# A third row buffer in the raw slots of the last expert's weights, used from the fifth unit on

## The chip, the core and the metric

The kernel runs on one core of one Trainium2 chip. Its five engines (TensorE for matmuls, VectorE and ScalarE for element-wise work, GpSimd, which here issues indirect DMAs, and SyncE, which here issues plain DMAs and transposing loads) each take their instructions in a fixed order and wait for each other through semaphores. In the rows below they are PE (PEld: its weight loads), DVE, ACT, POOL and SP. The metric is the device time of one execution in microseconds (us); lower is better.

## What is computed

A causal convolution over 7 steps with softmax weights per head, and behind it a mixture of experts: each of 28672 tokens of width 192 goes to its two best of eight experts, with hidden width 1024.

```
w = softmax(weight)                                   # 8 heads, 7 taps
x = sum over k of w[h, k] * x_pad[:, s + k, h, :]     # 8 x 3584 tokens of 192
logits = x @ w_gate
noisy_logits = logits + log1p(exp(x @ w_noise)) * noise
top2, top2_w = two largest, softmax of the two
for e in range(8):
    h = maximum(x[mask] @ w1[e], 0.0)                 # 192 -> 1024
    out[mask] += top2_w[mask] * (h @ w2[e])           # 1024 -> 192
```

## The kernel before

**Units.** The tokens are cut into 28 units of 1024 (128 partitions by 8 tokens). A unit's way has four steps. Its x is loaded (`load_x`, two buffers) and convolved by the thread `conv`: 56 VectorE operations into `xc` (L574, L576; TensorE does it for the first units, L528). Then `xc` is scaled and written as two f16 parts, high and low, into a **row buffer** `rb`: ScalarE writes the high part (L599 and L601), VectorE the low part (L603 and L605). The thread `gating` transposes the rows (eight transposing DMAs on SP, L636, from unit 5 on), computes the logits (L651), picks the two experts, and writes weights and token number into the last columns of the same rows. Last, `scatters` sends every row to its place in two experts' lists in DRAM (`xs`): 16 indirect DMAs on GpSimd (L783). When the sixteenth has landed, the row buffer is free.

**Row buffers.** There are two (`NRB`), so unit u writes where unit u - 2 was. L595 and L596 tell the planner so (`mark("scattered", u - NRB)`), and on the chip L599 waits on the semaphores of those scatters. Each buffer has a pad that is set to zero once (L433).

**Blocks.** The other half of the work is 232 blocks: 29 rounds of eight experts. A block of 256 rows (128 in the first round) is loaded transposed from `xs` (`bT`, three buffers, L938 and L941 on SP), multiplied by w1 (L858, into `ph`), passed through relu into `h` (high part on ScalarE, L881; low part on VectorE, L885), multiplied by w2 (L895, 24 matmuls for 128 rows, into the one `py`), scaled by ScalarE into `y` (L902, six buffers) and added to the output by an indirect DMA on GpSimd (L907). One 128-row half is one y and one add. The adds of a block wait until those of the block before have landed. A round needs the scattered rows of certain units, and a small load of their numbers (L803) ahead of its first block.

**Order.** No engine's order comes from the code as it stands. A planner (`Plan`) runs all these parts as threads against estimated durations, and records an instruction on its engine when its thread is the next to go. `conv` and `gating` have an urgency that grows as the unit's round comes near (`due`); the scatters are spread out over time on purpose (at most 2.6 us plus 1.4 us each). A thread that meets a mark not yet set stands still in the plan.

**Weights.** Each expert's weights are loaded raw in four parts and split into an f16 high and low part (`split_weights`, L424 on ScalarE and L426 on VectorE). The slots form two chains: the split of one part is written into the slot in front of its raw one (`parts`). `slots1` and `slots2` have 17 slots each, of 1024 and 768 f32 per partition, and the two in the last places hold raw weights of the last expert only. Behind its split they are not used again.

Of the kernel before, what the change touches and what calls it, by code (L numbers as in the profile page):

```python
# [8 lines left out]
F32 = mybir.dt.float32  # L9
F16 = mybir.dt.float16  # L10
# [8 lines left out]
P = 128  # L19
TU = 8  # L20
ROW = 400
ROWF = ROW // 2
# [110 lines left out]
def kernel(  # L133
# [12 lines left out]
    B, S, D = x.shape  # L146
    H, K = weight.shape
    G = D // H
    E, _, F = w1.shape
# [26 lines left out]
    const = ctx.enter_context(tc.tile_pool(name="const", bufs=1))  # L176
# [19 lines left out]
    V = nc.vector  # L196
# [41 lines left out]
    def pow2(mx, n, t, name):  # L238

        f = small.tile([P, n], I32, name=name + "f")  # L240
        s = small.tile([P, n], I32, name=name + "s")
        i = small.tile([P, n], I32, name=name + "i")
        V.tensor_scalar(f, mx.bitcast(I32), 23, None, op0=OP.logical_shift_right)
        V.tensor_scalar(f, f, -1, t + 254, op0=OP.mult, op1=OP.add)
        V.tensor_scalar(f, f, 1, 253, op0=OP.max, op1=OP.min)
        V.tensor_scalar(s, f, 23, None, op0=OP.logical_shift_left)
        V.tensor_scalar(f, f, -1, 254, op0=OP.mult, op1=OP.add)
        V.tensor_scalar(i, f, 23, None, op0=OP.logical_shift_left)
        return s.bitcast(F32), i.bitcast(F32)
# [13 lines left out]
    PE, DVE, ACT, SP, POOL = "PE", "DVE", "ACT", "SP", "POOL"  # L263
# [4 lines left out]
    def mark(*key):  # L268
        return marks.setdefault(key, Mark())

    def done(*key, after=0.0):
        plan.mark(mark(*key), after)
# [23 lines left out]

    HC = FC // 2
    winv = const.tile([P, E], F32, name="winv")
    slots1 = [const.tile([P, F], F32, name=f"w1s{n}") for n in range(2 * E + 1)]
    slots2 = [const.tile([P, HC * D], F32, name=f"w2s{n}") for n in range(2 * E + 1)]  # L300

    def parts(e, c):
        slots, n = ((slots1, 2 * e + c), (slots2, 2 * e + c - 2))[c // 2]
# [122 lines left out]
                V.scalar_tensor_tensor(lo, st, wscale[e][:, m:m + 1], hi, op0=OP.mult, op1=OP.subtract)  # L426
            done("split", e, m)

    NRB, NPE, NTR = 2, 3, 5
    rbs = []  # L430
    for i in range(NRB):
        rb = rpool.tile([P, TU, ROW], F16, name=f"rb{i}")
        V.memset(rb[:, :, 384:ROW], 0.0)  # L433
        rbs.append(rb)
    NPART = U // 2 if U % 2 == 0 else U
    nzt, cps, xcs, inv = {}, {}, {}, {}
    scat, zeroed = {}, []
# [121 lines left out]
    def conv():  # L559
        for u in range(U):  # L560
            turn["conv"], xc = u, None
            yield mark("x", u)
            if u:
                yield mark("halo", u)
            hs = range(H) if u >= NPE else range(HH, H) if u == 0 else range(0)
            for k in reversed(range(K)):
                for h in hs:
                    yield DVE, 0.25 if k == K - 1 else 0.33
                    if xc is None:
                        xc = xcs[u] = cpool.tile([P, TU, D], F32, name="xc")  # L570
                    src = xts[u][:, k:k + TU, h * G:(h + 1) * G]
                    dst = xc[:, :, h * G:(h + 1) * G]
                    if k == K - 1:
                        V.tensor_scalar(dst, src, wt[:, h, k:k + 1], None, op0=OP.mult)  # L574
                    else:
                        V.scalar_tensor_tensor(dst, src, wt[:, h, k:k + 1], dst, op0=OP.mult, op1=OP.add)  # L576
            for h0 in range(0, H if u < NPE else 0, HH):
                if (u, h0) != (0, HH):
                    yield mark("cps", u, h0)
                    yield ACT, 0.95  # L580
                    if xc is None:
                        xc = xcs[u] = cpool.tile([P, TU, D], F32, name="xc")
                    nc.scalar.activation(xc.rearrange("p t (h g) -> p h t g", g=G)[:, h0:h0 + HH],  # L583
                                         cps[u, h0][:, :, :TU * G].rearrange("p h (t g) -> p h t g", g=G), AF.Copy)
                    plan.freed(ph_ring)
            done("conv", u)
            yield DVE, 1.7
            am = small.tile([P, TU], F32, name="am")
            V.tensor_reduce(am, xc, axis=AX.X, op=OP.max, apply_absolute_value=True)  # L589
            yield DVE, 1.3  # L590
            xsc, xinv = pow2(am, TU, TX, "x")
            yield DVE, 1.7
            V.tensor_tensor(xc, xc, xsc[:, :, None].to_broadcast([P, TU, D]), op=OP.mult)  # L593
            inv[u] = xinv
            if u >= NRB:  # L595
                yield mark("scattered", u - NRB)  # L596
            rb = rbs[u % NRB]
            yield ACT, 1.1
            nc.scalar.activation(rb[:, :, 0:128], xc[:, :, 0:128], AF.Copy)  # L599
            yield ACT, 0.6  # L600
            nc.scalar.activation(rb[:, :, 256:320], xc[:, :, 128:192], AF.Copy)  # L601
            yield DVE, 1.2
            V.tensor_tensor(rb[:, :, 128:256], xc[:, :, 0:128], rb[:, :, 0:128], op=OP.subtract)  # L603
            yield DVE, 0.65
            V.tensor_tensor(rb[:, :, 320:384], xc[:, :, 128:192], rb[:, :, 256:320], op=OP.subtract)  # L605
            done("rows", u)

    def gating():
        for u in range(U):
            turn["gating"] = u  # L610
            yield mark("rows", u)
            xinv, rb = inv.pop(u), rbs[u % NRB]
            rbf = rb.bitcast(F32)
            xT = None
            if u:
                yield from zeros_and_noise(u)
# [78 lines left out]
            for k in range(2):  # L695
                m = small.tile([P, TU], F32, name=f"m{k}")
# [395 lines left out]
    plan.spawn(halos(), 0.3)  # L1092
    plan.spawn(conv_pe(), 0.2)
    plan.spawn(conv(), wanted("conv", 70.0))
    plan.spawn(prepare_gates(), 0.3)
    plan.spawn(scale_weights(), wanted_weights("scale", 12.0))
    for m in range(2):
        plan.spawn(split_weights(m), wanted_weights(m, 6.0))
    plan.spawn(gating(), wanted("gating", 45.0))
    plan.spawn(block_loads(), 1.5)  # L1100
    plan.spawn(run_blocks())
# [60 lines left out]
```

## Time and profile before

| | us |
|---|---|
| three timed runs | 2024.60, 2022.66, 2016.06 |
| median | 2022.66 |
| the profiled execution's own time | 2030.29 |
| its span in the trace | 2028.3 |
| TensorE busy | 1946.0 (96%) |
| VectorE busy | 1557.7 (77%) |
| GpSimd busy | 1263.0 (62%) |
| ScalarE busy | 804.2 (40%) |

The page gives for each engine the time in which at least one of its instructions ran. TensorE's matmuls overlap, so a group's length in the timeline is read from the start of one group to the start of the next. "Idle before" in the timelines is the time for which an engine stood still ahead of an instruction, with what ended it; a wait for several semaphores is put down to the one that came last by the profile, and where the engine named had long been done it was another, often a DMA. Mean granted clock of TensorE over the span: 0.986 of full speed.

### The profile page before, as it was taken

To read this page: it belongs to the slowest core of one execution; us is meant where nothing else is said; L and a number is where in the kernel's file an instruction comes from. 1 tells how busy PE (TensorE), PEld (TensorE's weight loads), DVE (VectorE), ACT (ScalarE), POOL (GpSimd) and SP (SyncE) were. 2 spreads that over 40 slices of the span, in tenths; PEclk is the share of its full clock that TensorE was granted. 3 is DMA by queue.
4 is the path that set the end of the run, shared out by engine and by line. 5 is a ranking of instruction groups with operands and counts; after the bars stand their busy time and mean duration, and the time that the engine had idled before them with its cause. 6 is when DMAs were issued, how large, how long until landed. Compare 5 with 4: busy or idle time off the path is not lost. (4 is left out here: it accounts for less than half of the span.)

```text
span 2028.3 us, 52446 instructions
## 1 busy us (share of the span) xinstructions
PE 1946.0 (96%) x21703; PEld 1785.3 (88%) x21703; DVE 1557.7 (77%) x4042; ACT 804.2 (40%) x1173; POOL 1263.0 (62%) x915
## 2 busy tenths in 40 slices
PE   7779999999999999999999999999989999999997
PEld 7668899898999999989989888899989999999996
DVE  7799899898998989989888887788778865333332
ACT  4464444333444444334433333334333333333332
POOL 0566776577666767676666667666666666633333
PEclk9889999999999999999999999999999999999999
DMA  8845566877787767677766676667766765444442
GB/s 242 220 101 102 111 130 116 151 134 117 130 138 133 121 116 140 117 134 127 133 122 111 113 131 124 115 112 125 115 115 96 115 113 91 85 59 64 58 58 37
DMA packets 521882, 236.99 MB, mean 117 GB/s; under 512 B 401304, under 2 KB 508824, under 8 KB 521505
## 3 DMA queue, kind: packets, MB, share of 16 engines
q1 hardware_dynamic: 433824, 142.72, 34.2%
q0 software_dynamic: 87200, 90.80, 30.0%
q8 instruction: 171, 2.80, 0.6%
q14 instruction: 79, 0.65, 0.1%
q10 hardware_dynamic: 608, 0.02, 0.0%
HBM read 40.12 MB, written 115.38 MB: 77 GB/s over the span
## 5 line engine op out<-in xcount | busy, mean ns | idle before, releaser
L907 POOL DMA_INDIRECT out_dram<-y,ids x456 | 762.8, 1673 | 534.5 <-ACT y L902 160.7
L858 PE MATMUL ph<-bT,w1s 128*128 128x256 f16 (+2 forms) x9280 | 994.3, 271 | 15.9 <-DMA bT<-xs 7.7
L895 PE MATMUL py<-w2s,h 128*128 128x192 f16 x10944 | 986.2, 247 | 22.4 <-ACT y L902 22.3
L895 PEld LDWEIGHTS <-h 128*128 128x128 f16 x10944 | 910.3, 98 | 61.1 <-issue 53.5
L858 PEld LDWEIGHTS <-w1s 128*128 128x128 f16 (+1 forms) x9280 | 786.5, 97 | 131.5 <-issue 40.3
L885 DVE SCALAR_TENSOR_TENSOR h<-ph,h 128x1024 f16<-128x1024 f32 (+1 forms) x464 | 557.8, 1202 | 340.1 <-ACT h L881 336.7
L881 ACT ACTIVATE h<-ph 128x1024 f16<-128x1024 f32 (+1 forms) x464 | 468.2, 1009 | 593.9 <-PE ph L858 577.5
L783 POOL DMA_INDIRECT xs<-rb,idx x448 | 498.5, 1113 | 212.3 <-issue 133.0
L576 DVE SCALAR_TENSOR_TENSOR xc<-xt,wt,xc 128x192 f32<-128x192 f32 x1224 | 420.3, 409 | 2.1 <-DMA xt<-zero 2.1
L902 ACT ACTIVATE y<-py,ga 128x192 f32<-128x192 f32 x456 | 191.8, 421 | 487.7 <-PE py L895 483.1
L528 PE MATMUL ph<-xt,dg 128*128 128x192 f32 x280 | 50.4, 339 | 13.9 <-DMA xt<-in_x_dram 11.7
L603 DVE TENSOR_TENSOR rb<-xc,rb 128x1024 f16<-128x1024 f32 x28 | 34.2, 1220 | 37.8 <-ACT rb L599 34.9
L528 PEld LDWEIGHTS ph<-xt,dg 128*128 128x128 f32 x280 | 47.4, 198 | 14.3 <-DVE dg L508 11.7
L599 ACT ACTIVATE rb<-xc 128x1024 f16<-128x1024 f32 x28 | 29.5, 1055 | 65.2 <-DMA xs<-rb,idx 35.2
L574 DVE TENSOR_SCALAR xc<-xt,wt 128x192 f32<-128x192 f32 x204 | 53.9, 328 | 1.3 <-DMA xt<-in_x_dram 0.7
L589 DVE TENSOR_REDUCE am<-xc 128x8 f32<-128x1536 f32 x28 | 48.9, 1748 | 4.2 <-ACT xc L583 3.7
L593 DVE TENSOR_TENSOR xc<-xc,xs 128x1536 f32<-128x1536 f32 x28 | 49.0, 1751 | 0.0
L687 DVE SCALAR_TENSOR_TENSOR t<-t,t 128x64 f32<-128x64 f32 x168 | 37.8, 225 | 5.3
L497 ACT ACTIVATE xt<-xt 128x1152 f32<-128x1152 f32 x27 | 31.2, 1154 | 0.0
L733 DVE TENSOR_REDUCE sums<-M 128x72 f16<-128x576 f16 x23 | 26.7, 1160 | 0.0
L651 PE MATMUL misc<-gparts,xT 128*128 128x32 f16 (+1 forms) x752 | 23.3, 174 | 1.4 <-DMA xT<-rb 1.4
L651 PEld LDWEIGHTS <-xT 128*128 128x128 f16 x752 | 22.7, 96 | 1.9 <-DMA xT<-rb 1.5
(142 smaller groups left out, 613.9 us busy)
## 6 DMA issues: line engine op xcount, KB each, us to landing
out_dram<-zero SPq DMA_DIRECT2D x28, 768.0 KB
xt<-in_x_dram SPq DMA_DIRECT2D x27, 768.0 KB
bT<-xs SPq DMA_TRANSPOSE x464
out_dram<-y,ids POOLq DMA_INDIRECT x456
xs<-rb,idx POOLq DMA_INDIRECT x448
w2s<-in_moe_w_dram SPq DMA_DIRECT2D x16, 384.0 KB
w1s<-in_moe_w_dram SPq DMA_DIRECT2D x8, 512.0 KB
w1s<-in_moe_w_dram SPq DMA_DIRECT2D x16, 256.0 KB
```

The source lines that it names most:

```text
L528: nc.tensor.matmul(c[:, h - h0, :TU * G].rearrange("p (t g) -> p t g", g=G), diag[h, k], xts[u][:, k:k + TU, h * G:(h + 1) * G], start=(k ...
L574: V.tensor_scalar(dst, src, wt[:, h, k:k + 1], None, op0=OP.mult)
L576: V.scalar_tensor_tensor(dst, src, wt[:, h, k:k + 1], dst, op0=OP.mult, op1=OP.add)
L589: V.tensor_reduce(am, xc, axis=AX.X, op=OP.max, apply_absolute_value=True)
L593: V.tensor_tensor(xc, xc, xsc[:, :, None].to_broadcast([P, TU, D]), op=OP.mult)
L783: s = nc.gpsimd.indirect_dma_start(out=xsf, out_offset=bass.IndirectOffsetOnAxis(ap=idx[:, k, t:t + 1], axis=0), in_=rbf[:, t, :], in_offs ...
L858: nc.tensor.matmul(ph[:, f, :T], w, x, start=opens and f // 2 not in banks[:i], stop=closes and f // 2 not in banks[i + 1:], skip_group_ch ...
L881: nc.scalar.activation(h[:, 0, half * nf:(half + 1) * nf, :T], ph[:, :, :T], AF.Relu)
L885: V.scalar_tensor_tensor(h[:, 1, hs, :T], ph[:, :, :T], 0.0, h[:, 0, hs, :T], op0=OP.max, op1=OP.subtract)
L895: nc.tensor.matmul(py[:, half, :D], h[:, a, f, ts], w2_part(e, lo, f), start=(n == 0), stop=(n == 3 * FC - 1), skip_group_check=True)
L902: nc.scalar.activation(y, py, AF.Copy, scale=gate)
L907: a = nc.gpsimd.indirect_dma_start(out=out, out_offset=bass.IndirectOffsetOnAxis(ap=ids, axis=0), in_=y, in_offset=None, compute_op=OP.add)
```

## The change

The two slots in the last places of `slots1` and `slots2` become two views of one tile, `last`, of 1024 + 768 f32 per partition. Its first 1600 f32 are a third row buffer, `rbs[2]`. Units 0 to 3 use the first two in turn, as before; from unit 4 on (`THIRD`) three are used in turn, beginning with the third. Unit 4 waits for the split of the last expert (both parts) and sets the pad to zero; unit u from 5 on waits for the scatters of unit u - 3.

```
-    slots1 = [const.tile([P, F], F32, name=f"w1s{n}") for n in range(2 * E + 1)]
-    slots2 = [const.tile([P, HC * D], F32, name=f"w2s{n}") for n in range(2 * E + 1)]
+    slots1 = [const.tile([P, F], F32, name=f"w1s{n}") for n in range(2 * E)]
+    slots2 = [const.tile([P, HC * D], F32, name=f"w2s{n}") for n in range(2 * E)]
+    last = const.tile([P, F + HC * D], F32, name="last")
+    slots1.append(last[:, :F])
+    slots2.append(last[:, F:])
...
+    rbs.append(tuple(last.bitcast(dt)[:, :TU * n].rearrange("p (t n) -> p t n", n=n) for dt, n in ((F16, ROW), (F32, ROWF))))
+
+    def rows_of(u):
+        return rbs[u % 2 if u < THIRD else (u - THIRD + 2) % 3]
+
+    def rows_before(u):
+        return u - 2 if u < THIRD else None if u == THIRD else u - 3
...
-            if u >= NRB:
-                yield mark("scattered", u - NRB)
-            rb = rbs[u % NRB]
+            if u == THIRD:
+                for m in range(2):
+                    yield mark("split", E - 1, m)
+            elif u >= 2:
+                yield mark("scattered", rows_before(u))
+            rb = rows_of(u)[0]
+            if u == THIRD:
+                yield DVE, 0.1
+                V.memset(rb[:, :, 384:ROW], 0.0)
```

Since the planner sets the order, the change moves instructions. In the changed kernel the lines have other numbers: L599 is L615 there, L601 is L617, L881 is L896, L902 is L917, L497 (the copy of x's halo) is L507. The first place is ScalarE at unit 8, with the semaphores that each instruction waits for (DMASW are those of GpSimd's indirect DMAs, DMAHW those of SP's DMAs). Before:

```order
L497 ACTIVATE xt<-xt 128x1152 [waits DMAHW5_49,DVE_49]
L881 ACTIVATE h<-ph 128x1024 [waits PE_49,Activation_49]
L902 ACTIVATE y<-py,ga 128x192 [waits DMASW7_49,PE_49]
L599 ACTIVATE rb_189<-xc 128x8x128 [waits DMAHW0_49,DMASW6_49,DMAHW1_49,DMASW5_49,DMAHW2_49,DMASW3_49,DMAHW3_49,DMASW2_49,DMAHW6_49,DMASW1_49,DMAHW7_49,DMASW0_49,DVE_49]
L601 ACTIVATE rb_189<-xc 128x8x64
L881 ACTIVATE h<-ph 128x1024 [waits PE_49]
L902 ACTIVATE y<-py,ga 128x192 [waits DMASW1_49,PE_49]
```

and of the changed kernel:

```order
L507 ACTIVATE xt<-xt 128x1152 [waits DMAHW5_49,DVE_49]
L896 ACTIVATE h<-ph 128x1024 [waits PE_49,Activation_49]
L917 ACTIVATE y<-py,ga 128x192 [waits DMASW7_49,PE_49]
L615 ACTIVATE rb_188<-xc 128x8x128 [waits DMAHW3_49,DMAHW4_49,DMAHW2_49,DMAHW6_49,DMAHW1_49,DVE_49]
L617 ACTIVATE rb_188<-xc 128x8x64
L896 ACTIVATE h<-ph 128x1024 [waits PE_49]
L917 ACTIVATE y<-py,ga 128x192 [waits DMASW1_49,PE_49]
```

Nothing has moved here; the copy into the row buffer has lost its waits for scatters, since ScalarE has by then waited for later DMAs of GpSimd in front of a y.

The second place is ScalarE at unit 25, from its halo copy (L507) to its copy into the row buffer. Before, the piece in front of the latter is:

```order
L718 ACTIVATE d<-d 128x8
L881 ACTIVATE h<-ph 128x1024
L902 ACTIVATE y<-py,ga 128x192
L881 ACTIVATE h<-ph 128x1024
L902 ACTIVATE y<-py,ga 128x192
L881 ACTIVATE h<-ph 128x1024
L902 ACTIVATE y<-py,ga 128x192
L881 ACTIVATE h<-ph 128x1024
L599 ACTIVATE rb_191<-xc 128x8x128
L902 ACTIVATE y<-py,ga 128x192
L601 ACTIVATE rb_191<-xc 128x8x64
```

and of the changed kernel:

```order
L507 ACTIVATE xt<-xt 128x1152
L917 ACTIVATE y<-py,ga 128x192
L615 ACTIVATE last<-xc 128x8x128
L896 ACTIVATE h<-ph 128x1024
L617 ACTIVATE last<-xc 128x8x64
L917 ACTIVATE y<-py,ga 128x192
```

Counted from the start, 331 y stand ahead of the copy before and 326 in the changed kernel: it has moved forward by five halves of a block. The sixteenth scatter that it waits for has 330 adds ahead of it on GpSimd before (unit 23), and 314 in the changed kernel (unit 22); the scatters of a unit stand at the same place in both.

The third place is VectorE at unit 4, where the row buffer's low part is written (L603 and L605; L619 and L621 in the changed kernel). Before:

```order
L593 TENSOR_TENSOR xc<-xc,xs 128x1536
L885 SCALAR_TENSOR_TENSOR h<-ph,h 128x1024
L603 TENSOR_TENSOR rb_189<-xc,rb_189 128x8x128
L605 TENSOR_TENSOR rb_189<-xc,rb_189 128x8x64
L574 TENSOR_SCALAR xc<-xt,wt 128x8x24
```

and of the changed kernel:

```order
L603 TENSOR_TENSOR xc<-xc,xs 128x1536
L900 SCALAR_TENSOR_TENSOR h<-ph,h 128x1024
L613 MEMSET last 128x8x8
L619 TENSOR_TENSOR last<-xc,last 128x8x128
L900 SCALAR_TENSOR_TENSOR h<-ph,h 128x1024
L621 TENSOR_TENSOR last<-xc,last 128x8x64
L584 TENSOR_SCALAR xc<-xt,wt 128x8x24 x7
```

The memset of the pad has come in, and an h stands one row earlier. Between unit 4 and unit 19 the engines' orders differ only in names and in such small steps of unit 4; from unit 19 on the steps of convolution and routing stand earlier, by up to five blocks at the end.

## Rows read from the trace of the kernel before

**Rows 1.** The page, its first part: busy time, share, instructions

```profile
PE 1946.0 (96%) x21703; PEld 1785.3 (88%) x21703; DVE 1557.7 (77%) x4042; ACT 804.2 (40%) x1173; POOL 1263.0 (62%) x915
```

**Rows 2.** Waits of TensorE, 390 to 1530 us: total, times, longest

```profile
PE py L895 <- ACT y L902: 18.8, 7, 5.4
PE ph L858 <- DVE h L885: 5.3, 3, 2.0
```

**Rows 3.** Timeline of ScalarE at unit 25: start, length, instruction [idle before <-releaser]

```profile
1517.61 1.06 ACT L599 ACTIVATE rb<-xc 128x1024 f16<-128x1024 f32 x1 [7.15 <-DMA xs<-rb,idx]
```

**Rows 4.** Timeline of GpSimd: the sixteenth scatter of unit 23

```profile
1512.58 0.98 POOL L783 DMA_INDIRECT xs<-rb,idx  x1 [0.30 <-issue]
```

**Rows 5.** Timeline of TensorE around seven stalls; last, a window of it (clock third)

```profile
403.86 2.14 PE L895 MATMUL py<-w2s,h 128*128 128x192 f16 x24 [1.72 <-ACT y L902]
405.84 1.91 PE L858 MATMUL ph<-bT,w1s 128*128 128x256 f16 x16
...
468.70 3.39 PE L895 MATMUL py<-w2s,h 128*128 128x192 f16 x24 [3.65 <-ACT y L902]
471.89 2.36 PE L858 MATMUL ph<-bT,w1s 128*128 128x256 f16 x16
...
874.59 2.14 PE L895 MATMUL py<-w2s,h 128*128 128x192 f16 x24 [1.86 <-ACT y L902]
...
1055.75 3.38 PE L895 MATMUL py<-w2s,h 128*128 128x192 f16 x24
1058.92 2.39 PE L858 MATMUL ph<-bT,w1s 128*128 128x256 f16 x16
...
1182.92 3.71 PE L895 MATMUL py<-w2s,h 128*128 128x192 f16 x24
...
1316.17 3.64 PE L895 MATMUL py<-w2s,h 128*128 128x192 f16 x24 [3.55 <-ACT y L902]
...
1519.03 4.00 PE L895 MATMUL py<-w2s,h 128*128 128x192 f16 x24 [5.37 <-ACT y L902]
1522.82 2.54 PE L858 MATMUL ph<-bT,w1s 128*128 128x256 f16 x16
...
1521.00:1522.00 1.00, 1.00 (x8) 0.50 0.19 34
```

**Rows 6.** Timeline of ScalarE at unit 9

```profile
521.92 1.06 ACT L599 ACTIVATE rb<-xc 128x1024 f16<-128x1024 f32 x1
```

**Rows 7.** One line's instructions: times, ns least/median/most, first and last start

```profile
L433 DVE MEMSET rb<- x2: 112/112/112, 7.1 to 7.2; 128x64 uint32 x2
```

**Rows 8.** Timeline of ScalarE: the y of numbers 75, 79, 219 and 255

```profile
442.92 0.42 ACT L902 ACTIVATE y<-py,ga 128x192 f32<-128x192 f32 x1 [0.90 <-PE py L895]
...
459.03 0.42 ACT L902 ACTIVATE y<-py,ga 128x192 f32<-128x192 f32 x1 [1.18 <-DMA out_dram<-y,ids]
...
1035.31 0.42 ACT L902 ACTIVATE y<-py,ga 128x192 f32<-128x192 f32 x1 [0.90 <-PE py L895]
...
1190.40 0.42 ACT L902 ACTIVATE y<-py,ga 128x192 f32<-128x192 f32 x1 [0.95 <-PE py L895]
```

**Rows 9.** Timeline of GpSimd: the adds of numbers 75, 219 and 255

```profile
463.24 1.59 POOL L907 DMA_INDIRECT out_dram<-y,ids  x1 [1.37 <-issue]
...
1050.03 1.60 POOL L907 DMA_INDIRECT out_dram<-y,ids  x1 [0.30 <-issue]
...
1192.80 1.65 POOL L907 DMA_INDIRECT out_dram<-y,ids  x1 [1.38 <-issue]
```

**Rows 10.** Windows: length, busy of PE, PEld, DVE, ACT, POOL, clock, DMA, GB/s

```profile
500.00:850.00 350.00, 350.00 (x3952) 321.49 (x3950) 319.54 (x852) 142.69 (x209) 242.08 (x182) 1.00 0.73 128
1190.00:1520.00 330.00, 318.33 (x3550) 291.24 (x3548) 268.92 (x702) 126.75 (x186) 221.21 (x158) 0.99 0.67 117
```

**Rows 11.** Windows, GpSimd's adds (L907) alone: length, busy and count, clock, DMA

```profile
500.00:850.00 350.00, 142.87 (x87) 1.00 0.73 128
1750.00:1950.00 200.00, 77.85 (x50) 1.00 0.46 63
```

More of the change, by code (lines that the diff above doesn't have):

```diff
@@ L427, in split_weights @@
             done("split", e, m)
-    NRB, NPE, NTR = 2, 3, 5
+    NPE, NTR, THIRD = 3, 5, 4
     rbs = []
-    for i in range(NRB):
+    for i in range(2):
         rb = rpool.tile([P, TU, ROW], F16, name=f"rb{i}")
         V.memset(rb[:, :, 384:ROW], 0.0)
-        rbs.append(rb)
+        rbs.append((rb, rb.bitcast(F32)))
+    rbs.append(tuple(last.bitcast(dt)[:, :TU * n].rearrange("p (t n) -> p t n", n=n) for dt, n in ((F16, ROW), (F32, ROWF))))
[3 more added lines that the diff above has]
+        return u - 2 if u < THIRD else None if u == THIRD else u - 3
     NPART = U // 2 if U % 2 == 0 else U
@@ L611, in gating @@
             yield mark("rows", u)
-            xinv, rb = inv.pop(u), rbs[u % NRB]
-            rbf = rb.bitcast(F32)
+            xinv, (rb, rbf) = inv.pop(u), rows_of(u)
             xT = None
```

## The prediction

> **What bounds the kernel now.** I read the page's first part, the waits of TensorE, the timelines around one stall on each engine, the queues of ScalarE and GpSimd side by side, and last the windows. TensorE is busy 1946.0 us of a span of 2028.3 [rows 1]: 82 us is all that any change off TensorE can give, and part of it lies in the start, which this change leaves alone. From 390 to 1530 us TensorE waits for two things only: for ScalarE to empty py, 18.8 us in 7 waits, and for VectorE's h, 5.3 us in 3 [rows 2]. The reader should then see that neither engine is slow there. Take the largest. ScalarE does nothing for 7.15 us and then starts L599, the copy into the row buffer, at 1517.61 [rows 3]; the y that TensorE needs stands behind it in ScalarE's order. What came last is a scatter issued at 1512.58 on GpSimd's queue [rows 4], the sixteenth of unit 23, whose buffer unit 25 wants: it ended there at 1513.56 and freed ScalarE 4.05 us later. TensorE idles 5.37 us and then runs 24 matmuls in 4.00 us instead of 2.14 [rows 5].
>
> **What the change takes away.** Each of the seven waits for y falls within 4 us of a late L599. So do the three for h, since VectorE's L603 stands behind L599 in the same way. Idle time: 18.8 + 5.3 = 24.1 us, in ten stalls.
>
> Five of the ten also cost clock. Around the restart the granted clock falls to 0.50, its lower level of 1.2 GHz: the group of 24 second-product matmuls that takes 2.14 us takes 3.39, 3.38, 3.71, 3.64 and 4.00, and the sixteen behind it, 1.91 us otherwise, take 2.36, 2.39 and 2.54 in three cases [rows 5]. That is 1.25 + 1.24 + 1.57 + 1.50 + 1.86 + 0.45 + 0.48 + 0.63 = 9.0 us. Together 33.1 us.
>
> Does the new order end these waits? From unit 5 on the copy of unit u waits for the scatters of u - 3. Counted in the order's rows, it stood 0.5 to 3 blocks behind the last scatter that it needs (units 7 to 27); now it stands 4.5 to 10.5 behind, and a block takes some 8 us (232 blocks in a span of 2028.3). What was late were a few us. What is late next on ScalarE is then nothing L599 waits for: the copy of unit 9 started with no idle time already [rows 6], as did seven others, and TensorE has no stall beside them.
>
> **What it adds.** One memset of the pad in the third buffer, on VectorE at unit 4: L433 did the same in 0.112 us [rows 7], beside TensorE's work; uncovered it costs 0.1 us. Unit 4 waits for the split of the last expert's weights instead; that split stands over 100 rows ahead of the new memset on VectorE, so it has long run. SP's loads of that expert keep their places, two of them into the joined piece. The small steps of unit 4's routing shift by a few rows against its h, and nothing there is waited for now: 0, within 1 us either way.
>
> **What it moves.** From unit 19 on the planner finds a free buffer sooner: convolution, routing, and on SP the transposes, zeros, noise and x loads go forward by 0.5 to 5 blocks; the scatters on GpSimd keep their places. VectorE then does a unit in about 7.3 blocks instead of 8. That pace stands in the trace: from 500 to 850 us VectorE is busy 319.54 of 350 us, 91%, and TensorE does not idle at all; from 1190 to 1520 VectorE has 268.92 of 330, 81% [rows 10]. I cost the move at 0; if VectorE does not keep up, that is rival 4. The loads on SP ahead of the blocks' transposes have the same neighbours as in units 5 to 18, at the same pace, so 0 as well.
>
> **What is given back.** GpSimd's queue is the part I would not cost at nothing. The y written at 442.92 is added at 463.24 [rows 8, 9]; both are number 75 in their queues, so the add starts 19.9 us after the y is done. There are six y buffers, so ScalarE can be only about 20 us ahead: at 459.03 it waits 1.18 us for an add [rows 8]. At 1035.31 (number 219) the lag is still 14.3 us, and at 1190.40 (number 255) 2.0 [rows 8, 9]. An add that starts 14 us late does not wait for its y, so over that stretch the queue runs at its own pace, and the stalls are part of what kept TensorE from running away from it. Without them its lead grows by what was removed so far: before 1035 by 1.72 + 3.65 + 1.70 + 1.86 = 8.9 us [rows 5], and 14.3 + 8.9 = 23.2 is 3 more than six buffers allow. By 1190 another 5.3 idle and 3.3 of clock are gone, 17.5 in all, and 2.0 + 17.5 is within them. So 3 us come back as short waits for y, too short for the clock to fall, as with 1.72 and 1.86 us [rows 5]. Bounds: 0, if the matmuls behind each y absorb it; 18.6, if the queue never catches up behind 1190 either, so that the other 33.1 - 17.5 = 15.6 us are lost too. I take 3: from unit 17 on the order has 2.0 scatters to a block instead of 2.2, which spares the queue some 0.2 to 0.3 us a block.
>
> The Trainium skill speaks against this in SBUF — State Buffer, "SBUF: two separate sides": GpSimd's descriptor writing stands still while certain VectorE instructions hold a port that both share. The trace agrees weakly: an add takes 142.87 / 87 = 1.64 us where VectorE is at 91%, and 77.85 / 50 = 1.56 where it has little to do [rows 11]. By that, 0.08 us on two adds of some 45 blocks would be 7 us more on GpSimd, which is off the path unless rival 1 holds.
>
> **Sum.** 24.1 + 9.0 - 3.0 - 0.1 = 30.0 us. The profiled execution took 2030.29 us (the span and 2 us around it); less 30.0 that is 2000.3. It stands 7.6 us above the median of 2022.66. Taken off the median, 30.0 gives 1992.7; if the profiled execution was longer only by more of these very stalls, every run ends at 2000.3. I forecast between the two: 1996, 1.3% less.
>
> **Rivals.** (1) GpSimd's queue binds to the end: 33.1 - 18.6 - 0.1 = 14.4 off 2022.66, 2008. For it: a lag of 14 us as late as 1035. Against: fewer scatters to a block later, and a lag of 2 at 1190.
>
> (2) Only the idle time comes back, since the timed runs had few of the clock's falls: 24.1 - 3.1 = 21.0 off, 2002. For it: five of ten stalls show no fall, those of 1.72 and 1.86 us among them [rows 5]. The Trainium skill, in TensorE: Matmul & The Clock Gate, "What's actually happening", says that the point at which the gate acts varies from run to run; the trace agrees in that half of the stalls show it.
>
> (3) The change does not do what it says: the planner uses the third buffer to run ahead and then stands at the next scatter as before, or the two weights' slots in one piece bring a wait of their own. 2022. Against: the places counted above.
>
> (4) Slower: VectorE falls behind from unit 19 on. It is idle 30.5 of 350 us at the pace it would then have [rows 10], some 5 us to a unit; if a unit's work grows by more, h comes late in each of nine units. At the price of the largest stall, 5.37 + 1.86 + 0.63 = 7.9 us each, 71 us are lost: 2022.7 - 30.0 + 71 = 2064. It outweighs the gain from 3.3 us a unit on. Against: the same density runs clean for 350 us.
>
> **How the numbers follow.** Forecast 0.60, (1) 0.17, (2) 0.11, (3) 0.07, (4) 0.05. A measurement of this kernel can tell about 0.5%, 10 us, from no change; faster is under 2012.5. The forecast, (2) and nearly all of (1) lie there: 0.86. (3) and the rest of (1) are within: 0.09. Slower: (4), 0.05. The range reaches from the quickest run shown less all 33 us, 2016.06 - 33 = 1983, to a little above (1), 2011.
>
> **What would show it.** Right: in the profile of the changed kernel the copies into the row buffer have no idle time behind a scatter; TensorE's waits for y and h between 390 and 1530 us shrink from 24.1 to some 3; the granted clock does not fall behind 160 us; adds start near 20 us after their y from 430 to 1190. Wrong: many waits of about 1 us for y up to 1700 (rival 1), waits for h behind VectorE after 1180 (rival 4), copies that still wait for scatters (rival 3), or an unchanged count of clock falls.

## The result and the profile after

On the chip that timed both, the kernel before took 2029.69 us (median of 20 runs, 2016.06 to 2041.69) and the changed kernel 2012.0 us (20 runs, 2006.39 to 2019.4): a ratio of 0.9906, 95% interval 0.9888 to 0.9924, so 0.9% faster. Laid on the 2022.66 us of the front table that is 2003.6 us, where 1996 was forecast. The profiled execution took 2008.07 us against 2030.29: 22.2 us less, where the sum said 30.0; the two medians stand 17.7 us apart.

The line of the page that answers to [rows 1]:

```profile
PE 1941.1 (97%) x21703; PEld 1782.5 (89%) x21703; DVE 1558.4 (78%) x4043; ACT 804.8 (40%) x1173; POOL 1245.1 (62%) x915
```

The waits of TensorE from 390 to 1530 us (total, times, longest), which answer to [rows 2]:

```profile
PE py L910 <- DVE h L900: 4.1, 1, 4.1
```

The ten stalls are gone: no wait for y is left there and one for h, which is a new one. ScalarE shows why. First the copy's line in the kernel before, grouped from 390 to 1530 us (busy, mean ns, then the idle time ahead of it and what ended it):

```profile
L599 ACT ACTIVATE rb<-xc 128x1024 f16<-128x1024 f32 x19 | 20.1, 1055 | 48.7 <-DMA xs<-rb,idx 35.2 <-DMA bT<-xs 7.8 <-DMA nzt<-in_moe_noise_dram 5.3
```

The same line after, where the buffer can also be `last`:

```profile
L615 ACT ACTIVATE rb<-xc 128x1024 f16<-128x1024 f32 x12 | 12.6, 1053 | 1.2 <-DVE xc L603 1.0
L615 ACT ACTIVATE last<-xc 128x1024 f16<-128x1024 f32 x7 | 7.4, 1051 | 0.6 <-DVE xc L603 0.6
```

35.2 us of waiting for scatters became none, and the 13.1 us put down to loads went with them. The unit of [rows 3], which had 7.15 us of idle time ahead of its copy, now starts it with none:

```profile
1473.45 1.05 ACT L615 ACTIVATE last<-xc 128x1024 f16<-128x1024 f32 x1
```

The windows of [rows 10], after (VectorE is the third busy time):

```profile
500.00:850.00 350.00, 350.00 (x3950) 321.42 (x3948) 321.14 (x849) 142.74 (x210) 237.54 (x180) 1.00 0.76 128
1190.00:1520.00 330.00, 330.00 (x3735) 303.03 (x3730) 294.29 (x785) 133.41 (x196) 226.72 (x164) 1.00 0.69 123
```

From 1190 to 1520 us VectorE went from 81% to 89%, and TensorE, which had idled 11.7 us there, idles not at all. But one place got worse. TensorE's timeline near 376 and 417 us (start, length, instruction, idle time ahead and what ended it):

```profile
376.67 0.24 PE L666 MATMUL misc<-gparts,xT 128*128 128x32 f16 x3 [2.33 <-DMA xT<-rb]
...
417.04 1.78 PE L910 MATMUL py<-w2s,h 128*128 128x192 f16 x10 [4.14 <-DVE h L900]
418.61 4.39 PE L873 MATMUL ph<-bT,w1s 128*128 128x256 f16 x28
```

The windows there (length, busy, granted clock, DMA share, GB/s):

```profile
375.00:400.00 25.00, 22.83 (x238) 0.93 0.69 157
400.00:425.00 25.00, 20.86 (x206) 0.86 0.76 150
```

TensorE stands 2.33 and 4.14 us, and 28 matmuls that take 2.67 us nearby take 4.39. What is late stands on three engines. First VectorE's timeline, then that of SP's queue:

```profile
414.11 0.19 DVE L837 COPY_PREDICATED idf<-ok,mt 128x16 f32<-128x16 int32 x1 [7.22 <-DMA mt<-xs]
```

```profile
409.63 1.01 SPq L818 DMA_DIRECT2D mt<-xs  x2
```

The waits of GpSimd, and of SP's queue, between 340 and 420 us:

```profile
POOL xs L798 <- DMA xs<-zero: 17.6, 3, 6.9
...
SPq L469 <- DMA xs<-rb,idx: 14.3, 3, 6.1
...
SPq L818 <- DMA xs<-rb,idx: 6.5, 1, 6.5
```

VectorE waits 7.22 us for the numbers of the next round (mt). Their load on SP (L818) waits for unit 5's scatters, and those wait on GpSimd, 17.6 us in three places between 340 and 420 us, for SP's writes of zero rows (L469), which in turn wait 14.3 us for scatters: the two queues take turns. The kernel before had the same (15.7 us in three, and 4.8 us of VectorE's waiting for mt), beside the late copy that led to the stall at 403.86 [rows 5]. The copy was the later one of two; with it gone the other shows.

How the 22.2 us come about can be counted in matmuls. TensorE from the start to 160, to 425 and to 1950 us (length, busy time and number of matmuls, granted clock, DMA share, GB/s), in the kernel before:

```profile
0.00:160.00 160.00, 118.69 (x1302) 0.91 0.71 184
0.00:425.00 425.00, 378.00 (x4249) 0.97 0.69 147
0.00:1950.00 1950.00, 1880.46 (x20986) 0.99 0.66 120
```

and after:

```profile
0.00:160.00 160.00, 117.91 (x1274) 0.89 0.72 182
0.00:425.00 425.00, 373.33 (x4134) 0.95 0.68 145
0.00:1950.00 1950.00, 1898.33 (x21233) 0.99 0.67 121
```

The changed kernel is 28 matmuls behind at 160 us, 115 behind at 425 and 247 ahead at 1950. At the 11.1 to a microsecond that the two traces run at, it loses 3 us at the start and 8 at this place, and gains 33 from there to 1950. The 33 are near what the sum has for that stretch, 33.1 less the 1.72 of the stall at 403.86. At the start TensorE's first waits for DMAs came out a little longer (the one for zeros in xt 3.2 us against 2.1). Executions of one order of work differ there by more: the run with the memory alone, below, whose order is that of before, has 1258 matmuls done at 160 us. So those 3 are put down to chance.

### The profile page after: what moved, and what is told of

Same layout as the page of the kernel before. It is cut to its first block, busy times and chain, and to the rows that moved or that the text cites. A ratio compares the mean times of both kernels' runs of the same rounds, so it can differ in the third digit from the quotient of the medians.

```text
span 2006.1 us, 52422 instructions
## 1 busy us (share of the span) xinstructions
PE 1941.1 (97%) x21703; PEld 1782.5 (89%) x21703; DVE 1558.4 (78%) x4043; ACT 804.8 (40%) x1173; POOL 1245.1 (62%) x915
## 4 chain that ended last, share of the span: by engine, by line
PE 94%; DVE 2%; DMA 2%; SPq 1%; issue 0%; POOL 0%; ACT 0%; DVEq 0%; POOLq 0%
PE ph L873 45%; PE py L910 45%; PE ph L538 2%; PE misc L666 1%; PE misc L380 1%; SPq L651 0%; DVE w1s L429 0%; POOL out_dram L922 0%; DMA xs<-rb,idx 0%; PE ph L642 0%; DVE w2s L429 0%; DMA xt<-in_x_dram 0%; DMA xt<-zero 0%; DMA gst<-in_moe_w_gate_dram 0%; DMA mt<-xs 0%
## 5 line engine op out<-in xcount | busy, mean ns | idle before, releaser
L922 POOL DMA_INDIRECT out_dram<-y,ids x456 | 755.0, 1656 | 526.8 <-DMA out_dram<-y,ids 148.4
L896 ACT ACTIVATE h<-ph 128x1024 f16<-128x1024 f32 (+1 forms) x464 | 467.8, 1008 | 612.9 <-PE ph L873 590.1
L798 POOL DMA_INDIRECT xs<-rb,idx x320 | 352.7, 1102 | 176.0 <-issue 93.4
L917 ACT ACTIVATE y<-py,ga 128x192 f32<-128x192 f32 x456 | 191.4, 420 | 489.6 <-PE py L910 486.2
L798 POOL DMA_INDIRECT xs<-last,idx x128 | 135.8, 1061 | 39.0 <-issue 37.5
L599 DVE TENSOR_REDUCE am<-xc 128x8 f32<-128x1536 f32 x28 | 49.0, 1749 | 4.2 <-ACT xc L593 3.6
L603 DVE TENSOR_TENSOR xc<-xc,xs 128x1536 f32<-128x1536 f32 x28 | 49.0, 1752 | 0.0
L507 ACT ACTIVATE xt<-xt 128x1152 f32<-128x1152 f32 x27 | 31.2, 1154 | 0.0
L615 ACT ACTIVATE rb<-xc 128x1024 f16<-128x1024 f32 x20 | 21.1, 1054 | 16.5 <-DVE lim L830 6.1
```

The lines of the kernel that those rows point to most:

```text
L798: s = nc.gpsimd.indirect_dma_start(out=xsf, out_offset=bass.IndirectOffsetOnAxis(ap=idx[:, k, t:t + 1], axis=0), in_=rbf[:, t, :], in_offs ...
L896: nc.scalar.activation(h[:, 0, half * nf:(half + 1) * nf, :T], ph[:, :, :T], AF.Relu)
L917: nc.scalar.activation(y, py, AF.Copy, scale=gate)
L922: a = nc.gpsimd.indirect_dma_start(out=out, out_offset=bass.IndirectOffsetOnAxis(ap=ids, axis=0), in_=y, in_offset=None, compute_op=OP.add)
```

## The experiments

Each job ran its kernels on one chip beside the kernel before: 2038.82 us there in the first job, 2039.54 in the second, 2036.41 in the third. All ratios are to the kernel before of the same job.

**The changed kernel again, twice.**

> The changed kernel once more, as the measure for the three beside it. Theory (the ten stalls behind the copy into the row buffer are gone; what is missing is one new stall around 376 to 420 us, where VectorE waits for the load of round 5's numbers, behind the scatters of unit 5, which wait for the writes of zero rows): some 18 us faster than before, and in its profile again one stall of TensorE of 3 to 6 us between 370 and 425, and none from 430 to 1950. Rival (that stall was chance in one execution): no stall there.

> The changed kernel once more, as the base for the runs beside it on this chip: ratio 0.990 to 0.994 of the kernel before. Its waits for y are there in some executions (12.4 us in one, 3.6 us in another); the load of round 5's numbers or the transposes near 380 us cost a stall with a fall of the clock in each.

2020.87 us, ratio 0.9934 (0.9906 to 0.9962), and 2019.78 us, 0.9905 (0.9879 to 0.993). In these two profiled executions no stall of TensorE comes from the round's numbers: VectorE waits 2.2 and 2.5 us for them. TensorE stands a little earlier instead, for transposed rows (xT), 7.2 and 5.9 us in all. The longest such wait of the first of the two, and its SP queue, where a write of zero rows that waited for scatters stands in front of the transposes:

```profile
383.10 0.26 PE L666 MATMUL misc<-gparts,xT 128*128 128x32 f16 x3 [4.08 <-DMA xT<-rb]
```

```profile
365.95 0.64 SPq L469 DMA_DIRECT2D xs<-zero  x1
...
369.32 7.75 SPq L651 DMA_TRANSPOSE xT<-rb  x5
```

That no stall follows from 430 us on was expected, and missed: the two have waits for y that the first execution lacked. TensorE's waits from 390 to 1530 us in the first of the two:

```profile
PE py L910 <- ACT y L917: 12.4, 11, 2.4
```

In the second:

```profile
PE py L910 <- ACT y L917: 19.4, 14, 2.5
```

ScalarE's wait in the same stretch of the second, and one of its places in the timeline:

```profile
ACT y L917 <- DMA out_dram<-y,ids: 117.6, 51, 5.2
...
957.97 0.42 ACT L917 ACTIVATE y<-py,ga 128x192 f32<-128x192 f32 x1 [4.35 <-DMA out_dram<-y,ids]
```

ScalarE waits 117.6 us for an add to hand a y buffer back, against none in that stretch of the first execution. So the give-back through the six y buffers is real, and how much of it there is differs between executions of one program. These short waits for y cost no clock in the second profile: the granted clock from 390 to 1530 us is 1.00 there.

**The memory alone, no third buffer in use.**

```
-    NPE, NTR, THIRD = 3, 5, 4
+    NPE, NTR, THIRD = 3, 5, 1000
```

> The last expert's raw weights made one piece of memory, as in the change, but no unit uses it as a row buffer: two row buffers as before, and the order of the work as before. Own theory: the third buffer is the whole of it, so this is as the kernel before, ratio 0.998 to 1.002, with ScalarE's waits for scatters, some 35 us in all, still there. Rival: the place of the memory alone (one piece in place of two tiles from the weights' pool) brings part of the gain, ratio below 0.997.

2043.58 us, ratio 1.0016 (0.9995 to 1.0038): no change. ScalarE's waits for scatters are there as before:

```profile
ACT rb L615 <- DMA xs<-rb,idx: 44.9, 12, 7.1
ACT y L917 <- DMA out_dram<-y,ids: 43.7, 19, 4.7
```

One piece of memory neither brings nor costs anything that can be measured; the buffer does. The second line shows that the waits for adds do not come from the change alone: with two row buffers ScalarE waits 43.7 us for them in this execution, and 2.1 us in the trace that the prediction was read from.

**The third buffer, but the planner held to the old distance.**

```
-            elif u >= 2:
-                yield mark("scattered", rows_before(u))
+            if u >= 2:
+                yield mark("scattered", u - 2)
```

> The third buffer, but the planner still holds unit u back until the scatters of unit u - 2, so that every instruction behind unit 4 stands where it stood before. Theory (the wait of the copy is what cost time): the same as the changed kernel within 4 us, some 2012, no wait of ScalarE for a scatter ahead of the copy. Rival (the forward move of convolution and routing from unit 19 on gives the gain): only the stalls up to unit 18 go, 14 of 33 us, and the time is 12 us or more above the changed kernel's.

2017.18 us, ratio 0.9912 (0.9882 to 0.9942), beside 0.9934 for the changed kernel in the same job: not to be told apart. The rival's loss of 12 us or more is not there; what moving units 19 to 27 forward gives, if anything, is too small to be seen. What gains is that the copy waits for an older unit's scatters.

**The zero rows freed, after and before.** The writes of zero rows and the scatters of units 0 to 5 go to different rows; here neither waits for the other.

```
+            for v in scat:
+                if reach[v + 1] <= lo_row:
+                    tc.declare_no_dep(z.ins, group=f"scat{v}", reason="rows ahead of the zeros")
+            tc.add_to_no_dep_group("zero rows", z.ins)
...
+            if reach[u + 1] <= lo_row:
+                tc.declare_no_dep(s.ins, group="zero rows", reason="rows ahead of the zeros")
```

> The changed kernel with the writes of zero rows and the scatters of units 0 to 5 free of each other (their rows differ); the order stays. Theory: GpSimd's three waits for the zeros (17.6 us) go, the load of round 5's numbers comes in time, the stall between 370 and 425 goes: 7 to 10 us less than the changed kernel, some 2003, and the adds run later than their y by less than 10 us instead of 11 to 17. Rival (the lag of the adds comes from GpSimd's own load): lag as before from 450 on, and the time within 3 us of the changed kernel.

> The kernel before with the same freeing of the zero rows, two row buffers. Theory (the copy waits since the order has it only 0.5 to 3 blocks behind its last scatter; the lag of the adds from the zeros adds to that): the stalls at units 7 and 8 (7 us) go, those from unit 15 on shrink but stay, 2010 to 2023. Rival (the zeros alone made GpSimd late, and with it the copies): all ten stalls go and the time falls to some 2000, with no third buffer.

After: 2011.37 us, 0.9871 (0.9828 to 0.9913). Before: 2026.3 us, 0.9953 (0.9922 to 0.9983). In both the stalls between 370 and 470 us are gone, which settles their cause. In the kernel before, those from unit 15 on stay, 14.9 us for y and 8.4 for h; they were 18.7 us in the first trace, so they did not shrink as was expected. In the changed one, ten waits for y take the place of the early stalls. Nor did the adds come nearer to their y: under 10 us was expected, and between 600 and 1200 us they start 14 to 24 us after it, where they started 12 to 17 after it in the first execution of the changed kernel. On that point this execution agrees with the rival: the adds are late without the zero rows too. TensorE's waits from 390 to 1530 us in the kernel before with the zero rows freed:

```profile
PE py L902 <- ACT y L909: 14.9, 4, 5.8
PE ph L865 <- DVE h L892: 8.4, 3, 4.3
```

TensorE's and ScalarE's in the changed kernel with the zero rows freed, same stretch:

```profile
PE py L917 <- ACT y L924: 13.4, 10, 1.8
...
ACT y L924 <- DMA out_dram<-y,ids: 92.0, 39, 4.4
```

**Ten y buffers**, alone and with the zero rows freed (the order of the work stays):

```
-        y = ffn[0].tile([P, D], F32, name="y", bufs=6)
+        y = ffn[0].tile([P, D], F32, name="y", bufs=10)
```

> The changed kernel with ten buffers for y in place of six, and the same order on every engine. In one execution of the changed kernel the matrix engine waited at eleven places between 477 and 1139 us for a y, 12.4 us in all, and ScalarE waited 82 us in 38 places for adds to hand a y buffer back (1.5 us in another execution of the same program). Theory A: six y buffers are what is left on the path behind the change; with ten, ScalarE's wait for the adds falls under 10 us, the eleven stalls go, and the time falls by 8 to 12 us against the changed kernel on the same chip, to a ratio near 0.987 of the kernel before. Theory B: the adds are late as such (GpSimd's queue can't keep up there), and ten buffers only put the wait off: the lag of the adds grows from 20 to over 30 us and the stalls stay, ratio 0.991 to 0.993.

> The changed kernel with ten y buffers and with the writes of zero rows and the scatters of units 0 to 5 free of each other: both leftovers taken away. If the two are the only ones (A), no wait of the matrix engine over 1 us is left between 160 and 1950 us, the clock stays at 1.00 there, and the ratio to the kernel before is 0.980 to 0.984 (freeing the zero rows alone gave 0.9871, and ten waits for y of 13.4 us stood in its profile). If the adds are late as such (B), it comes out at 0.987 like the freeing alone.

> The changed kernel with ten y buffers and the zero rows freed, once more, on this chip: ratio 0.983 to 0.989 of the kernel before, as the first time (0.9863), which puts it in front of the changed kernel (0.9905 to 0.9934) by 4 to 13 us. If the first time was luck, 0.990.

Alone: 2024.39 us, ratio 0.9927 (0.9905 to 0.9949), no better than the changed kernel beside it (0.9905). TensorE's waits for y shrink from 19.4 to 2.8 us, as theory A said (ScalarE's for adds only from 117.6 to 49.2, where A had under 10), and the lag grows, as B said: number 150's y on ScalarE and its add on GpSimd stand 40 us apart, where they were 24 us apart in the changed kernel beside it. Then the load of a round's numbers, which waits for scatters that stand behind those adds, is late at 1206 us. The timelines of the y and its add:

```profile
758.86 0.42 ACT L917 ACTIVATE y<-py,ga 128x192 f32<-128x192 f32 x1
...
798.85 1.62 POOL L922 DMA_INDIRECT out_dram<-y,ids  x1 [1.65 <-ACT y L917]
```

VectorE and TensorE at 1206 us, with ten buffers:

```profile
1206.21 0.19 DVE L837 COPY_PREDICATED idf<-ok,mt 128x16 f32<-128x16 int32 x1 [10.75 <-DMA mt<-xs]
...
1208.77 1.78 PE L910 MATMUL py<-w2s,h 128*128 128x192 f16 x10 [8.78 <-DVE h L900]
```

Many waits under 2.5 us were traded for one of 8.78 us and the fall of the clock behind it. Neither theory had that.

Both together: 2008.72 us, 0.9863 (0.9832 to 0.9893), and again 2003.07 us, 0.987 (0.983 to 0.991). No wait for y is left in either profile between 390 and 1530 us, yet the ratio is the one that theory B named, and A's 0.980 to 0.984 was not reached. By its ratios this is the quickest version. Weighted by their intervals, its two ratios make 0.9866 and the changed kernel's three (0.9906, 0.9934, 0.9905) 0.9912: a difference of 0.0046, 0.0019 to 0.0073. Against the freed zero rows alone (0.9871) it is not told apart. The second profile shows the whole stretch (length, busy of the five engines, granted clock):

```profile
390.00:1530.00 1140.00, 1139.94 (x12845) 1047.44 (x12844) 1027.45 (x2720) 464.32 (x678) 785.88 (x577) 1.00 0.74 126
```

TensorE runs through 1140 us at full clock. The first profile had two waits for h there, 4.2 us.

**More work for GpSimd**, in the changed kernel and in the one before:

```
     def add_rows(j, ids, y, adds):
+        for _ in range(2):
+            nc.gpsimd.iota(jp, pattern=[[1, P]], base=0, channel_multiplier=-1)
         apart()
```

> The changed kernel with two small iotas (128x128, 0.23 us each in the profile's first microseconds) on GpSimd ahead of every add. Between 425 and 1500 us of the changed kernel GpSimd's 548 instructions took 743 us, 0.3 us lay ahead of most of them, and most of the rest, some 150 us in 80 places, are adds that wait although their y is over 10 us old, so for another add's landing. Theory A: GpSimd's queue is what the kernel stands at behind the change. Then 267 adds at 0.5 to 0.8 us more, some 130 to 210 us, less what lies in those 150 us, push the adds to the limit of the six y buffers, and the time grows by 20 to 100 us, with PE's idle time waiting for y. Theory B: GpSimd has room enough; the time grows by under 8 us.

> The same two iotas ahead of every add in the kernel before. Its ScalarE waits let GpSimd catch up at each of the ten stalls (the adds' lag fell to 1 to 3 us behind them). Theory A: the extra work costs here about as much as in the changed kernel, so that the change gains little with it, under 10 us between the two. Theory B: it costs under 8 us in both.

2149.08 us, ratio 1.0582 (1.0524 to 1.064), and 2162.5 us, 1.0652 (1.0594 to 1.0709). GpSimd was busy 1480.7 us in place of 1245.1 in the first and 1487.9 in place of 1263.0 in the second, 225 to 236 us more; some 130 us of it came out at the end in both, above the 20 to 100 us that theory A had for the changed kernel. So GpSimd's queue has little room in either kernel. Whether the change gains under 10 us with the load, as was expected, can't be told: the medians stand 13.4 us apart, with intervals of 12 us to each side. The changed kernel with the load, GpSimd's groups from 425 to 1500 us:

```profile
L924 POOL DMA_INDIRECT out_dram<-y,ids x238 | 401.9, 1689 | 186.0 <-ACT y L917 68.9 <-issue 63.3 <-DMA out_dram<-y,ids 19.4
L922 POOL IOTA jp<- 128x128 int32 x476 | 143.9, 302 | 19.0
```

Its waits of TensorE (390 to 1530 us) and of ScalarE (425 to 1500):

```profile
PE py L910 <- ACT y L917: 80.6, 90, 2.8
...
ACT y L917 <- DMA out_dram<-y,ids: 408.5, 143, 5.5
```

The two main waits of ScalarE for DMAs in the kernel before with the load, 425 to 1500 us, and TensorE's for y, 390 to 1530:

```profile
ACT y L902 <- DMA out_dram<-y,ids: 108.0, 42, 4.8
ACT rb L599 <- DMA xs<-rb,idx: 75.2, 10, 11.8
...
PE py L895 <- ACT y L902: 69.1, 28, 10.0
```

With two row buffers a late queue stops ScalarE at the copies (75.2 us in ten) and at the y buffers (108.0 in 42), with three at the y buffers alone (408.5 us in 143): the same lateness, met in smaller pieces. The clock tells the pieces apart: the mean granted clock is 0.982 in all four runs of the changed kernel with the load, and 0.963 to 0.967 in those of the kernel before with it.

**The price of a stall.** ScalarE held 5.3 us longer at the copy, with no DMA in it:

```
-            nc.scalar.activation(rb[:, :, 0:128], xc[:, :, 0:128], AF.Copy)
+            for _ in range(6 if u >= 7 else 1):
+                nc.scalar.activation(rb[:, :, 0:128], xc[:, :, 0:128], AF.Copy)
```

> The changed kernel with the first copy into the row buffer done six times from unit 7 on (21 units): ScalarE holds 5.3 us more at the place where the kernel before waited for scatters, with no DMA in it. The prediction had ten stalls of the matrix engine at 24.1 us idle behind waits of 3.5 to 5.3 us, and 9.0 us of lower clock behind five of them, 3.3 us for each. Own theory: some 2 to 3.5 us for each of 21 units, 45 to 75 us in all, part of it as clock at a lower level behind the longer ones. Rival: the matrix engine has work enough in front of it and a late ScalarE is hidden, under 20 us in all; the gain then came from elsewhere (the scatters' place in GpSimd's queue).

2116.89 us, ratio 1.0413 (1.0351 to 1.0476), two runs. One of the delayed copies with the y behind it on ScalarE, and the stall that it makes on TensorE:

```profile
911.50 6.50 ACT L616 ACTIVATE rb<-xc 128x1024 f16<-128x1024 f32 x6 [0.96 <-DVE xc L603]
917.90 0.40 ACT L918 ACTIVATE y<-py,ga 128x192 f32<-128x192 f32 x1
...
918.35 4.00 PE L911 MATMUL py<-w2s,h 128*128 128x192 f16 x24 [4.61 <-ACT y L918]
```

TensorE's waits from 390 to 1720 us:

```profile
PE py L911 <- ACT y L918: 65.9, 18, 4.6
PE ph L874 <- DVE h L901: 10.0, 4, 3.6
```

75.9 us of idle time, 3.6 for each of 21 units, and groups of 24 matmuls of 3.1 to 4.0 us, in place of 2.14, behind most of them. With the changed kernel at 0.9905 to 0.9934 (in the other two jobs) the delay costs 0.048 to 0.051 of 2036 us, 97 to 103 us, 4.6 to 4.9 for each unit, above the 45 to 75 us of the expectation. A late ScalarE is not hidden there. The clock's part is read from 390 to 1720 us, first in this run, then in the second repeat of the changed kernel:

```profile
390.00:1720.00 1330.00, 1253.98 (x13667) 0.97 0.66 116
```

```profile
390.00:1720.00 1330.00, 1310.61 (x14733) 1.00 0.72 122
```

A clock that is 0.03 lower over 1330 us is some 40 us, or 1.9 for each unit. The idle time is not all added either: GpSimd catches up in these stalls, and ScalarE's wait for adds, 81.7 and 117.6 us in the two repeats, is 4.8 us here, so that the 12.4 and 19.4 us of TensorE's waits for y that the repeats have go. 75.9 less these is 57 to 64 us, and with the 40 that makes the 97 to 103. So the clock adds more than half as much again to the idle time.

## Why the prediction was right, and where its size was off

**What bounds the kernel, and that the change ends it: right.** The ten waits were the copies' waits for scatters. With the third buffer ScalarE waits for no scatter; with the memory alone it does, and the time is that of before; a copy that is late for another reason makes the same stalls. The argument from places in the order (4.5 blocks of distance where 0.5 stood) held.

**Idle 24.1 and clock 9.0: right in what they hold.** All ten stalls went, and their five falls of the clock with them. That a stall costs clock beside its idle time, 33.1 us for ten, fits the delay experiment: 4.6 to 4.9 us for each unit delayed by 5.3, some 1.9 of it clock, where the waits behind the ten were often shorter.

**What it adds and moves, 0: right for the memory, the memset and the move from unit 19 on.** Rival 4 had VectorE fall behind there; it is busy 89% of 1190 to 1520 us and TensorE idles 0.

**But that nothing else was late was wrong at one place.** It had no term in the sum, and so was put at 0. The writes of zero rows were on GpSimd's queue in the trace of before, 15.7 us of waits just ahead of the first two stalls [rows 5], and the text asked "what is late next" of ScalarE alone, not of VectorE. The next one there was the load of a round's numbers. In the first profile this place gave back 8 us of 33, with two falls of the clock behind 160 us, where the text said that there would be none; in the repeats it was the transposes behind the same writes. The zero rows freed take both away, and the early stalls of the kernel before too.

**The 3.0 given back by GpSimd's queue was the mis-sized term of the sum.** The mechanism (add behind y, six buffers, ScalarE waits) is what the repeats show, but at 12.4 and 19.4 us of TensorE's waits between 390 and 1530 us, and at 0 in the first execution. The step that failed took the lag in one trace, 14.3 us at 1035.31, and added to it what was removed, as if the queue went on at a pace of its own. The traces and the added load point to a queue so near its limit that its lag does not settle by such a sum: from 600 to 1200 us it is 12 to 17 us in the first execution, 12 to 23 in the two repeats, and 29 to 40 with ten buffers. The sign that the adds would start near 20 us after their y from 430 to 1190 us was thus missed in the first execution (9 to 17 us). What sets the difference between executions of one program stays open, and the order of before has such waits too (43.7 us of ScalarE's with the memory alone). Rival 1 (this queue binds to the end, 2008) was therefore nearer than its 0.17 said: its mechanism shows in both repeats, with waits of up to 2.5 us, though most of them end by 1110 us.

**Rival 2 came nearest in number, 2002, and is not what happened.** It had only the idle time come back, since the timed runs had few of the clock's falls. They had them: the mean granted clock of the kernel before is 0.986 in its profiled execution, and 0.981 to 0.989 in its 27 runs of the first job; in the twenty runs of the changed kernel it is 0.985 to 0.992. Clock did come back, and other losses took its place.

**The size.** The prediction did not know whether to take its 30.0 off the median of three runs, 2022.66, or off the profiled execution, 2030.29, and chose between the two. The twenty runs settle it: their median is 2029.69, so the three lay low by chance and the profiled execution was an ordinary one. 30.0 off 2029.69 is 1999.7, and 2012.0 was measured, 12.3 us more. 8 of these are of the size of the place at the zero rows, and the rest of that of the waits for y in the repeats; how they divide in the timed runs is not shown. Choosing 1996, below the profile's own sum of 2000.3, added to the miss: on the base of 2022.66 the ratio puts it at 2003.6.

**The sentence on the port that VectorE and GpSimd share** (the Trainium skill, SBUF — State Buffer, "SBUF: two separate sides"), 7 us more on GpSimd: no run here isolates it. The 130 us that the load cost only suggest that such an amount would not have been wholly off the path, where the text put it.

## What to carry over

When a buffer is added to end a wait, list every wait that ended shortly before the one removed, on every engine that the stalled one needs: the second latest is the new bound, and a wait that costs nothing today can cost once the later one is gone. A queue that stays far behind what feeds it, as the adds here start 12 us and more after their y, may be near its limit; more buffers in front of it move the wait on to whatever stands behind it in that queue (here the scatters, and the loads that need them), so take work or needless order off the queue before adding buffers. Here the third buffer paid, and the zero rows freed paid on top of it (0.9871); ten y buffers brought no gain that can be seen, neither without the freeing (0.9927) nor with it (0.986 to 0.987).

## What the runs showed that was not expected

The waits for y of one program differ between executions by more than any part of this change but the main one: ScalarE's wait for adds was 0, 81.7 and 117.6 us from 390 to 1530 us.

A short idle time can bring the lower clock where a longer one does not. In the delay experiment 2.29 us stand ahead of 24 matmuls that take 3.48 us, at 984.02, and 3.54 us ahead of 24 that take 2.14 us, at 1706.48. The granted clock of such a restart can't be read from the idle time alone.

The added iotas took 302 ns each from 425 to 1500 us and 226 at the start, where one stood alone. They took longer late in the kernel, 460 ns (49.74 us for 108) from 1850 to 2050 us, where VectorE was busy 64.77 of 200 us; why is open.
